# A skip term moved from VectorE to TensorE, a refolded argmax, a split load and a new order of steps

## The chip, the cores and the metric

The kernel runs on one core of a Trainium2 chip. The metric is device time of one execution in microseconds; the time of a kernel is the median of its runs. The engines are PE (TensorE), DVE (VectorE), ACT (ScalarE), POOL (GpSimd) and SP (SyncE, which only issues DMAs here). PSUM is the memory that PE writes its results to; DVE and ACT read it.

## What is computed

An input x of 2048 rows by 448 channels is normalised by rows (xn). The output is the sum of three terms:

```python
xn = layernorm(x)
return x + A(xn) + B(xn)

# A: a state-space convolution, per channel d, with 256 states n
P = exp(dt * A[d, n] * l)                    # l = 0 .. 2047
K = real(einsum("dn,dnl,dn->dl", C, P, dt * B))
A(xn) = causal_convolution(xn, K) + xn * Dskip

# B: a product-key mixture of 4096 experts, 16 heads, the best one of each head
q = einsum("nd,dhc->nhc", xn, w_q); s1 = q[..., :256] @ k1.T; s2 = q[..., 256:] @ k2.T
e = argmax(s1) * 64 + argmax(s2)             # 64 keys each; the softmax over one is 1
B(xn) = sum over heads of gelu(xn . u[e]) * v[e]
```

## The kernel before, in words

The kernel is written as streams of steps. Each step has an engine and a function that issues its instructions, and names the steps that it needs and the buffers that it takes and gives back. A string ORDER, one character a step, gives the order in which all steps are issued (`Plan.run`); each engine executes its own instructions in that order, and each waits by semaphores for what it needs. The steps carry planned costs, which issue nothing.

- **Weights.** `combine` folds w_q with the keys: 16 heads, loads wq from DRAM on SP, PE products `wc` (L889), transposes, ACT copies into W.
- **Layer norm and scores.** `ln` normalises tiles of 128 rows. `score` transposes a tile (L970), PE forms the scores of 32 lists of 64 keys (`sc`, L988 and L997), DVE takes the maximum of each list (L1012) and marks with 0 where an entry equals it (L1019, `eq`, in bf16). The argmax (stream sc_w) is then found by subtracting the ramp (64 - j)/128 from every entry (L1027) and by taking the minimum of the two halves three times, 64 to 32 to 16 to 8 entries (L1030), with a last reduction (L1033). The indices go to DRAM and come back (`ig`).
- **The convolution's kernel.** `batch` and `products` work on 8 channels at a time, 56 batches. DVE makes integer phases (L637, L641), ACT takes sines and cosines (L656 to L662, `CS`) and exponentials (L617, L619, `mg`), DVE multiplies them (L687 to L693, `zi` and `mg`). ACT's functions of different kinds need a table load when the kind changes. Then step k1 on PE sums over the states: for two groups of four channels, matmuls of 128 x 32 weights, which use a quarter of PE's columns each, into the PSUM tile `kp` (L709). Step k2 on ACT copies columns up to j0 = 63 of each group to `kt` (L717). Step k2b on DVE writes the last column, which holds time 0, as kp plus Dskip, since a skip term is an addition to the convolution's first tap (L720). `dsk` holds Dskip on partitions 0, 32, 64 and 96 and zeros elsewhere. Step k3 on PE takes the first Fourier stage of kt (`vp`, L729), and k4 on ACT copies it to VK (L733).
- **Convolution.** `conv` multiplies in the frequency domain for four chunks of channels (128, 128, 128, 64): PE `U` (L825), ACT, DVE `cp` (L835), PE `ip` (L857), ACT `tq`, stored to `t_d`.
- **Experts.** `experts`: for 64 groups, four indirect gathers by POOL bring rows of u and v (L1110, `ue`), DVE forms the dot products (L1118), ACT and DVE the gelu, PE the weighted sum `po` (L1148). ACT copies it (L1159), POOL adds it into the output in DRAM by an accumulating DMA (o_st, L1162).
- **Last stage.** `final`: `tl` is loaded from `t_d` on SP (L1188), PE applies the last stage (L1200). For the first three chunks POOL adds the result into the output (f_st, L1214). For the last chunk, SP loads the output's sums so far in one DMA, `bb` (L1180), when all 16 tiles of the experts have been stored; DVE adds the four parts (L1204), and SP stores them (L1212). SP's order at the end is three loads tl, the load bb, the fourth load tl, four stores.

The constants are loaded by SP at the start (`consts`): `dsk` by four DMAs of one row each (L332), after a POOL memset of the tile (L285).

Of the kernel before, what the change touches and what calls it, by code (L numbers as in the profile page):

```python
# [115 lines left out]
class Plan:  # L116
# [61 lines left out]
    "KKKKKSyy55TTTKhhghh7PQRZyyy5666UU56667iK9KSSTSSKKLLKK56mnjkUUUTTSSPQ59988KizdeTSTTSSAzzz!T#lT!$$5UKU5UTKK$%yyyMN5UUUTTKK"
    "iKUKK56UTSSTT955z5KUMRNZOyhSPQTTKzzz!VKUUUK#!W9$$WXSSTSUU5$%yyShhhKKK5545TTT45MNiiiiiiSThMRNZSPQz4KTTyjzhhAmnTUKklzz!SST"
    "gAAAAByyMNhhLLUKKSSYOyU#!ghhUUTTUUTUSUVmnzxzxi$$$%yyyyghhhiiiTjKMRNZOybTzxz!xSTTPQ#!UjSk$$KKKKKUcc$%yyffzzfUSTUWfMUTzz!z"  # L180
    "#!&SSTNMRZkSWXNO$fhhhhzllgKKKKKKKLLK$YYYSPQTTK$yzyz!mnTTT%yhimnKKyfSShhhgUUUU#Tz!$$SK$%fKUTTTUhhgUUhfKKfUVKzyyyyyyKzz!zx"
    "#!WhSSSPQ$$iTWK$%yyMTTiiizxSTfazxzx!dceUK#!(UK$i$SSST$%NMRZUUUTTzzSyzyyXYiiTThhhNMOyyKjiiklTS&(NMRZNOyKLPzTT!#!mnjUKUQgz"
    "klU$$$YShiihhhi%yyMNhhUSKKUTSUKzzzTTMRZNOKKULmni!#!UUVgh$$KSSThK$%WbzzKKTyzyyyzghKiihhMNSMNOTTfK!#yyTf!$UjPQRZS$zxklmnjf"
    "fU$%yyyyUUUfhWXzxzxzx!ST#!gKKKi$TKKKLLK$SSK$%yyyhhhhhhhfTTzzzffSTMNSz!TTkl&MNOKKKghhPQRTi#!fghhSS$$zzKU$%zUUfUTSSyyyyyyz"
    "!z#!KKdcebh$$UTUSSTUTTUUV$%yzzzTT!#!KK$TzxzxWmniPQSSUyyihhhy$$%yyUiiiyyUzxzxUTKUTK!#!ST$WXjkl$zSS$%yyyy&ihhmnTT(zzTzz!#!"
    "zhST$KT$zKjkgh$%yMUayyz!lmffhgUUU#!KUU$$NMRyz$%yyyyhhgNOKLKLPQMNUfffiiizzzzx!#!hhUUViiii$SMRNOyyzzz$xxxhhhhSSSTW!#!njk$T"
    "T$%yyyylmnSiihhhjkg$TT$%MNyyy&((zfflmnzzz!ffhhiiMNOSYYYWX#zzfgTT!$yz$ThPQRSz!$%yyyyUUb#iUUzzzhgST!$$$SoSz!jkUTTYYi#!hSTT"
    "Soooopzxzxzxhhdechhh$%yyyTpTTiiihj$l$%zx!i#!U$$qrpqrpooUkhfyyyy$%iqrqrzzhfffiaghhfpqpqyyyyyzlUUUUsrriizUtghhpqr!#gpqroUU"
    "!$$$jthiiVWhhhhhzzzzzusttuiiipqrpqr!#jklzz&(Yhhh%yy!pqrpoqrghhppqq$$$%IIIIIIIIghhfffffbklsrrtpqtzghhyyyiiiiWX!#!$$poqmnm"
    "nmmnn4ii$hzxzxzx4rrjjkkll%yyy5555udehihhhiimmnnzx!#siiighfhf!$$$6656jklmii%azzzfffyzyzyttu))hhgnj48899h&hghhgklm!#77777A"  # L190
    "66!$$$%yyyn*)6569885555599AAc5(zzhhiihhhihff+h6z!f*+#!z$$$%yyy)z,yhh55,yzghhg*ffbiiiiihhhdechhjiklmjn5554A55+,yg44AAByyy"
    "yyhhzz!#!xiklm$$$%yyyyhffffiiiihiin*hhg+,yjfhhgklmhhhhzxzxzx!#niizhhiijgklj!$$$%yyyyhiihfffffhhhghmhnghiabzzhdecz!zz#zzk"
    "&(lmijhhii!!$#$$z%yyyyzzznghhihhfklh!$$!#!mnijihhghkff$%yyyy$zzz$xz!#!hfghhh$%yyyy$lmfhhhiiijiingz$$%yyyyxxzklmxhizzzzzh"
    "hfnpp&(ijii!#hqrpYYklfqrpozf!$!#!$$%yyyyqqahg$$$%hhghhiirpqrpqdeczzzzzx!#ffbasrprpozxzxzxjg!$hhhii$$ttuhhkl!#yyyyqrpqrp!"
    "$$$hf%yyyy%yqhhhghhiiiiiffffq&(jklghhhhhhsrpttrpozzzzzzqii!#yyyijg!$$qrprphhfhzz!i$%#i!$hhgu$$%fffyqqhhgyzzzzzx!#!$$klsr"
    "prpofab$%iiiiyyyyyyyyyyhhhhhhttuzxzxzxqrqrhdehffffmnmnmn!#!$$$jkljgkli%yyyy&(mnmniiiiifhhhiimnsttughhjjzzzzz!#!$$$klklmn"
    "ghhzzzz!#!$$$zzzcm%yyy)%)yyyhhhhhiizxzx!#nigiiij!$$$hhihhgfff%yyklmhhnzxzxighhf!#!$$$*)+,yydefbajgklzzzzhhhhhiiiii*+hhfi"
    "%)yyym!#f&njhhghh*f(zzffklg!$$$%yyyy+zzmhhhhhiijii*klm!#,yhhzz+ngn,yiiiij!$$$%yyyyhffhiihhklghhmnzz!#!$jfffba$ghhgzxzxkl"
    "mhhiihhihhnhh$%yyyyzxijzx!ffif#!fhgklmizh$$$%yyyyhghhn&iijkgfzzz!zz#!$lmhnpp,yz$$%yyyyz!#!$$zzz$%yyyy(hiihhiihjqrpqrpohf"
    "ffhhhgz!zxqqrphhghqrpsqffbzx#!k$$$%yyyyzxzx!lhhdehhhii#!rpqrpoqiihiijgk$$$%&(tturpqrpsqzzzz!zrpyyhfhhhgf#!rpozzz!ihhgq$$"  # L200
    "$%qyyyyyyh#!hhiijkiif$$$%yyyttufzfhhhihjkihhrrppzzz!llglzxzxzxfqqs#!hhghfffftrrppozx!iihgqq#!hh$$$%iitu$$$zzzmnjklmnmnii"
    "hhhhyyyyyrrmn%&yyyy(ihhhiiiimnvovojiikliz!z#!$$$ismntjkl%wwyyyzzz!zzjkltuvmn#!$$$mnzv%ww))pprrpsrrpz!#!$$$ttusrttu%rsrrz"
    "zzz!#!$$$-*)ttusttu%&(*)*///+*+++:.;/:;:;:;<<<<,,,,")


class Kernel:
# [21 lines left out]
    def alloc(s):  # L228
# [25 lines left out]
        s.dsk = c.tile([128, D // 4], F32, name="dsk")  # L254
# [20 lines left out]
    def consts(s):  # L275
# [54 lines left out]
        def dsk():  # L330
            for c in range(4):
                s.nc.sync.dma_start(s.dsk[32 * c:32 * c + 1], io["dskip"][c:c + 1])  # L332
        s.dskip_done = p.add("c_ld", "SP", xf(4, 448), dsk, n=4, deps=[x0])
# [340 lines left out]
    def products(s, b, B, e_, c1, c2, VK, col, u):  # L674
# [24 lines left out]
        def k1():  # L699
# [3 lines left out]
            for gi in range(G):  # L703
                n = 0
                for t in range(2):
                    for ri in range(2):
                        for c in range(4):
                            m = 32 * (NB * t + 4 * gi + c)
                            s.nc.tensor.matmul(kp[32 * c:32 * c + 32, 64 * gi:64 * gi + 64], T[ri][:, 1024 + m:1056 + m],  # L709
                                               view(T[ri], m, [[512, 2], [1, 32]]), start=(n == 0), stop=(n == 3))  # L710
                        n += 1


        j0 = JB[0]

        def k2():
            s.nc.scalar.activation(B["kt"].rearrange("p (g j) -> p g j", g=G)[:, :, :j0], B["kp"].rearrange("p (g j) -> p g j", g=G)[:, :, :j0], AF.Copy)  # L717

        def k2b():
            s.nc.vector.tensor_tensor(out=B["kt"].rearrange("p (g j) -> p g j", g=G)[:, :, j0], in0=B["kp"].rearrange("p (g j) -> p g j", g=G)[:, :, j0],  # L720
                                      in1=s.dsk[:, G * b:G * b + G], op=ALU.add)
# [563 lines left out]
```

## Time and profile before

| | us |
|---|---|
| median of 3 runs | 867.54 |
| lowest and highest | 866.99, 868.65 |
| the profiled execution | 872.34 |
| its span, first to last instruction | 870.6 |

The profile is of one execution of its own, which is a little longer than the runs that were timed. A group's row has: line, engine, operation, what it writes and reads, shapes, count; then the busy time, the mean of one in ns, and the idle time of its engine just before, with what ended it. PE's tile shape stands before the shapes as rows*columns of the array. A busy PE counts each matmul from its start to its modelled end, so that overlapping ones are not counted twice.

### The profile page before, as it was taken

How to read it: one execution, taken by the hardware profiler on the slowest of the kernel's cores; microseconds unless marked ns; L12 is line 12 of the kernel's file. 1: busy time of each engine (PE TensorE's matmuls, PEld its weight loads, DVE VectorE, ACT ScalarE, POOL GpSimd, SP SyncE). 2: the span in 40 equal slices, each digit the busy share in tenths (PEclk: the TensorE clock that was granted, in tenths of full speed). 3: DMA queues.
4: the chain of work that ended last, by engine and by line, in shares of the span. 5: the costliest groups of instructions: out<-in, count | busy, mean ns of one | idle time of the engine just before them, and what ended most of it. 6: DMA issues, size and time to landing. Idle time of an engine off the chain costs nothing. (4 is left out here: it accounts for less than half of the span.)

```text
span 870.6 us, 19849 instructions
## 1 busy us (share of the span) xinstructions
PE 701.5 (81%) x7628; PEld 377.4 (43%) x7628; DVE 712.7 (82%) x1802; ACT 525.4 (60%) x962; POOL 350.6 (40%) x317
## 2 busy tenths in 40 slices
PE   3799999899999997988887475778876657877892
PEld 1234444344334433333664243456553434555662
DVE  5436999998999998988999899899988877688740
ACT  3468772552536645643578878868667866576630
POOL 1100111342444445463244267673555745444411
PEclk9999999999999999799998556699896665799995
DMA  8995622577877868879878989899889977788879
GB/s 258 311 337 202 212 56 100 172 258 214 250 226 234 299 210 249 307 208 332 284 226 259 282 198 292 276 309 275 265 288 340 251 223 209 235 247 251 248 200 178
DMA packets 145639, 212.59 MB, mean 244 GB/s; under 512 B 45512, under 2 KB 127560, under 8 KB 145480
## 3 DMA queue, kind: packets, MB, share of 16 engines
q0 software_dynamic: 29120, 124.27, 46.1%
q1 hardware_dynamic: 116424, 87.05, 33.3%
q8 instruction: 60, 0.98, 0.4%
q14 instruction: 35, 0.29, 0.1%
HBM read 181.65 MB, written 33.29 MB: 247 GB/s over the span
## 5 line engine op out<-in xcount | busy, mean ns | idle before, releaser
L1110 POOL DMA_INDIRECT ue<-in_uv_dram,ig x256 | 300.7, 1175 | 349.8 <-PE po L1148 100.9
L988 PE MATMUL sc<-W,xt 128*128 128x512 f32 x384 | 178.8, 605 | 5.6 <-ACT xt L973 4.0
L1118 DVE SCALAR_TENSOR_TENSOR ue<-ue,xr 128x448 f32<-128x448 f32 x256 | 149.7, 625 | 0.0
L988 PEld LDWEIGHTS sc<-W,xt 128*128 128x128 f32 x384 | 69.8, 191 | 92.4 <-issue 85.0
L709 PE MATMUL kp<-mg 128*32 128x64 f32 x1792 | 77.2, 248 | 25.1 <-DVE mg L693 10.3
L1148 PE MATMUL po<-ue,A 128*32 128x448 f32 x512 | 77.0, 664 | 22.5 <-DVE A L1141 21.4
L709 PE MATMUL kp<-zi 128*32 128x64 f32 x1792 | 80.9, 245 | 13.6 <-issue 13.0
L709 PEld LDWEIGHTS kp<-mg 128*32 128x32 f32 x1792 | 51.4, 125 | 49.0 <-issue 22.0
L617 ACT ACTIVATE mg<-lg 128x512 f32<-128x512 f32 x112 | 61.2, 595 | 13.7 <-PE lg L606 13.0
L693 DVE TENSOR_TENSOR mg<-mg,CS 128x1024 f32<-128x1024 f32 x56 | 68.9, 1231 | 0.0
L689 DVE TENSOR_TENSOR zi<-mg,CS 128x1024 f32<-128x1024 f32 x56 | 68.9, 1230 | 0.0
L729 PE MATMUL vp<-f,kt 128*64 128x128 f32 x448 | 45.0, 334 | 28.2 <-DVE kt L720 14.9
L709 PEld LDWEIGHTS kp<-zi 128*32 128x32 f32 x1792 | 57.1, 127 | 22.3 <-issue 21.8
L641 DVE CUSTOM_DVE_ANT_0 ph<-st,ph 128x512 uint16<-128x512 uint16 (+2 forms) x84 | 65.2, 777 | 1.6
L656 ACT ACTIVATE CS<-ph 128x1024 f32<-128x1024 int32 x56 | 61.8, 1104 | 6.0 <-DVE mg L693 4.2
L662 ACT ACTIVATE CS<-CS,halfpi 128x1024 f32<-128x1024 f32 x56 | 64.3, 1147 | 1.4
L659 ACT ACTIVATE CS<-ph 128x1024 f32<-128x1024 int32 x56 | 62.3, 1112 | 0.0
L1012 DVE TENSOR_REDUCE mx<-sc 128x8 f32<-128x512 f32 x64 | 43.7, 682 | 18.2 <-PE sc L997 10.5
L825 PE MATMUL U<-VU,g 128*64 128x128 f32 x384 | 44.9, 301 | 12.5 <-DVE cp L835 6.0
L729 PEld LDWEIGHTS vp<-f,kt 128*64 128x64 f32 x448 | 29.8, 164 | 54.9 <-DVE kt L720 16.0
L687 DVE SCALAR_TENSOR_TENSOR zi<-mg,CS 128x512 f32<-128x512 f32 x56 | 40.4, 721 | 14.9 <-ACT CS L656 10.9
L1125 ACT ACTIVATE x<-dot 128x4 f32<-128x4 f32 x64 | 13.0, 202 | 58.3 <-DVE ue L1118 57.1
(217 smaller groups left out, 1262.7 us busy)
## 6 DMA issues: line engine op xcount, KB each, us to landing
wq<-in_wq_dram SPq DMA_DIRECT2D x32, 448.0 KB
xr<-xn_d SPq DMA_DIRECT2D x64, 224.0 KB
vu_d<-vst SPq DMA_DIRECT2D x64, 112.0 KB
VU<-vu_d SPq DMA_DIRECT2D x12, 512.0 KB
t_d<-tq SPq DMA_DIRECT2D x24, 256.0 KB
tl<-t_d SPq DMA_DIRECT2D x12, 512.0 KB
ue<-in_uv_dram,ig POOLq DMA_INDIRECT x256
xx<-in_x_dram SPq DMA_DIRECT2D x16, 224.0 KB
```

Of the source, the lines that this page charges most:

```text
L641: s.nc.vector.tensor_tensor(out=rw(n, 2 * n), in0=rw(0, n), in1=o["st"][:, k, b0:b0 + 2].rearrange("p b h m x -> p (b h m x)")[:, None].to ...
L656: s.nc.scalar.activation(CS[:, 1].rearrange("p (m r x) -> p m r x", r=16, x=2), four(s.ph), AF.Sin, scale=SC)
L659: s.nc.scalar.activation(B["CS"][:, 0].rearrange("p (m r x) -> p m r x", r=16, x=2), four(s.ph), AF.Abs)
L662: s.nc.scalar.activation(B["CS"][:, 0], B["CS"][:, 0], AF.Sin, scale=-SC, bias=s.halfpi)
L689: V.tensor_tensor(out=zi[:, 512:], in0=mg[:, 512:], in1=CS[:, 1], op=ALU.mult)
L693: V.tensor_tensor(out=mg[:, 512:], in0=mg[:, 512:], in1=CS[:, 0], op=ALU.mult)
L709: s.nc.tensor.matmul(kp[32 * c:32 * c + 32, 64 * gi:64 * gi + 64], T[ri][:, 1024 + m:1056 + m], view(T[ri], m, [[512, 2], [1, 32]]), start ...
L729: s.nc.tensor.matmul(vp[64 * ri:64 * ri + 64, 128 * gi:128 * gi + 128], B["kt"][:, 64 * gi:64 * gi + 64], s.f1[:, ri], start=True, stop=True)
L988: s.nc.tensor.matmul(B["sc", q].rearrange("p a b -> p (a b)"), B["xt"][:, i], w, start=(q % 2 == 0 and i == 0), stop=(q % 2 == 1 and i == 2))
L1110: s.nc.gpsimd.indirect_dma_start(out=ue, out_offset=None, in_=s.io["uv"], in_offset=bass.IndirectOffsetOnAxis(ap=s.IDX[t][:, c, g:g + 1].b ...
L1118: s.nc.vector.scalar_tensor_tensor(Q["ue", c][:, :D], Q["ue", c][:, :D], 1.0, B["xr", c], op0=ALU.mult, op1=ALU.mult, accum_out=Q["dot"][: ...
L1148: s.nc.tensor.matmul(B["po"][32 * c:32 * c + 32, :D], Q["A"][:, c], Q["ue", c][:, D:], start=(g == 0), stop=(g == 3))
```

## The change

1. The skip term. After the matmuls of k1 for a group of four channels, four more are issued into the same PSUM columns: the weights are four rows of the identity matrix taken with a stride (4 x 32, a single 1 each), the moving operand is one column of `dsk`, which is now 4 x 112. They add Dskip to column j0 of each channel. The DVE step k2b is gone, its stream too, and k2 copies all 128 columns. k1 now also waits for dsk and for the identity matrix. The memset is gone, and one DMA loads dsk in place of four.
2. The argmax. Each minimum is now one scalar_tensor_tensor instruction that adds n/128 to the upper half and takes the minimum with the lower half. The subtraction of the ramp is left for the first 8 entries of each list, after the three minima.
3. The sums so far of the last chunk are loaded in four DMAs, one for each part of four tiles; each waits for the expert stores of its own four tiles, and each addition for its own part. SP's order at the end is three loads tl, three parts of bb, the fourth load tl, the fourth part, four stores.
4. ORDER is new throughout (the letters of the streams behind k2b move up by one).

```diff
@@ -251,7 +250,7 @@
         s.halfpi = c.tile([128, 1], F32, name="halfpi")
         s.one = c.tile([128, 1], F32, name="one")
         s.dum = c.tile([128, 1], F32, name="dum")
-        s.dsk = c.tile([128, D // 4], F32, name="dsk")
+        s.dsk = c.tile([4, D // 4], F32, name="dsk")
         s.amt = c.tile([128, 2, 4], I32, name="amt")
         s.ph = c.tile([128, 16, 2, 2, M, 2], I32, name="ph")
         s.lc = c.tile([128, 96 * NB], F32R, name="lc")
@@ -282,7 +281,6 @@
         def sets():
             s.nc.gpsimd.memset(s.halfpi, HALF_PI)
             s.nc.gpsimd.memset(s.one, 1.0)
-            s.nc.gpsimd.memset(s.dsk, 0.0)
             for h in range(2):
                 for k in range(4):
                     s.nc.gpsimd.memset(s.amt[:, h, k:k + 1], k + 2 + 6 * h)
@@ -328,9 +326,8 @@
 
 
         def dsk():
-            for c in range(4):
-                s.nc.sync.dma_start(s.dsk[32 * c:32 * c + 1], io["dskip"][c:c + 1])
-        s.dskip_done = p.add("c_ld", "SP", xf(4, 448), dsk, n=4, deps=[x0])
+            s.nc.sync.dma_start(s.dsk, io["dskip"])
+        s.dskip_done = p.add("c_ld", "SP", xf(4, 448), dsk, deps=[x0])
         ld("f1", lambda: s.f1, 131e3, 25e3)
         ld("mask", lambda: s.mask, 16e3, 30e3)
         ld("e", lambda: s.e, 197e3, 60e3)
@@ -707,18 +704,16 @@
                         for c in range(4):
                             m = 32 * (NB * t + 4 * gi + c)
                             s.nc.tensor.matmul(kp[32 * c:32 * c + 32, 64 * gi:64 * gi + 64], T[ri][:, 1024 + m:1056 + m],
-                                               view(T[ri], m, [[512, 2], [1, 32]]), start=(n == 0), stop=(n == 3))
+                                               view(T[ri], m, [[512, 2], [1, 32]]), start=(n == 0), stop=False)
                         n += 1
 
-
-        j0 = JB[0]
+                j0 = 64 * gi + JB[0]
+                for c in range(4):
+                    s.nc.tensor.matmul(kp[32 * c:32 * c + 32, j0:j0 + 1], s.ident[:4, c::4],
+                                       s.dsk[:, G * b + gi:G * b + gi + 1], start=False, stop=True)
 
         def k2():
-            s.nc.scalar.activation(B["kt"].rearrange("p (g j) -> p g j", g=G)[:, :, :j0], B["kp"].rearrange("p (g j) -> p g j", g=G)[:, :, :j0], AF.Copy)
-
-        def k2b():
-            s.nc.vector.tensor_tensor(out=B["kt"].rearrange("p (g j) -> p g j", g=G)[:, :, j0], in0=B["kp"].rearrange("p (g j) -> p g j", g=G)[:, :, j0],
-                                      in1=s.dsk[:, G * b:G * b + G], op=ALU.add)
+            s.nc.scalar.activation(B["kt"], B["kp"], AF.Copy)
 
         def k3():
             if VK["t"] is None:
@@ -731,9 +726,8 @@
 
         def k4():
             s.nc.scalar.activation(VK["t"][:, :, col:col + NB], B["vp"].rearrange("p (c k) -> p k c", k=32), AF.Copy)
-        a = p.add("s4_k1", "PE", 1340, k1, deps=[v], take=("kv", "kt"), give=("zi", "mg"))
-        a1 = p.add("s4_k2", "ACT", ac(126), k2, deps=[a])
-        a = p.add("s4_k2b", "DVE", dv(2) + 4, k2b, port=False, deps=[a1, s.dskip_done], give=("kv",))
+        a = p.add("s4_k1", "PE", 1450, k1, deps=[v, s.dskip_done, s.C["ident"]], take=("kv", "kt"), give=("zi", "mg"))
+        a = p.add("s4_k2", "ACT", ac(128), k2, deps=[a], give=("kv",))
         a = p.add("s4_k3", "PE", 510, k3, deps=[a, s.C["f1"]], take=("kv",) if VK["taken"] else ("kv", "vk"), give=("kt",))
         VK["taken"] = True
         VK["last"] = p.add("s4_k4", "ACT", ac(256), k4, deps=[a], give=("kv",))
@@ -1024,10 +1018,11 @@
 
 
             def vb():
-                s.nc.vector.tensor_tensor(out=B["eq"], in0=B["eq"], in1=s.wt[:, None, :].to_broadcast([128, 32, 64]), op=ALU.subtract)
+                s.nc.vector.tensor_tensor(out=B["eq"][:, :, :8], in0=B["eq"][:, :, :8], in1=s.wt[:, None, :8].to_broadcast([128, 32, 8]), op=ALU.subtract)
 
             def vc(n):
-                return lambda: s.nc.vector.tensor_tensor(out=B["eq"][:, :, :n], in0=B["eq"][:, :, :n], in1=B["eq"][:, :, n:2 * n], op=ALU.min)
+                return lambda: s.nc.vector.scalar_tensor_tensor(B["eq"][:, :, :n], B["eq"][:, :, n:2 * n], n / 128, B["eq"][:, :, :n],
+                                                                op0=ALU.add, op1=ALU.min)
 
             def ve():
                 s.nc.vector.tensor_reduce(out=P["cm"][:, t % 2].rearrange("p a b -> p (a b)"), in_=B["eq"][:, :, :8], axis=AX.X, op=ALU.min)
@@ -1037,7 +1032,7 @@
                 x1 = p.add("sc_a", "ACT", 8 * 196, va, deps=[x1], take=("eq",) if q == 0 else (), give=give)
             else:
                 x1 = p.add("sc_v", "DVE", dv(512), va, port=False, deps=[x1], take=("eq",) if q == 0 else (), give=give)
-        x1 = p.chain("sc_w", "DVE", [(dv(2048, 2), vb), (dv(1024, 2), vc(32)), (dv(512, 2), vc(16)), (dv(256, 2), vc(8)), (dv(256), ve)],
+        x1 = p.chain("sc_w", "DVE", [(dv(1024), vc(32)), (dv(512), vc(16)), (dv(256), vc(8)), (dv(256, 2), vb), (dv(256), ve)],
                      deps=[x1, s.wt_done], give=("eq" if t < 15 else "tq",))
         if t % 2 == 0:
             return
@@ -1175,11 +1170,15 @@
                 H["h"] = s.flat("q", "hb", 1024).rearrange("p (x e) -> p x e", e=32)
                 s.nc.sync.dma_start(H["h"], s.io["h"])
 
-            def lb():
-                H["b"] = s.flat("q", "bb", 1024).rearrange("p (t d) -> p t d", d=w)
-                s.nc.sync.dma_start(H["b"], s.io["out"][:, :, d0:].rearrange("t p d -> p t d"))
+            def lb(g):
+                def f():
+                    if g == 0:
+                        H["b"] = s.flat("q", "bb", 1024).rearrange("p (t d) -> p t d", d=w)
+                    s.nc.sync.dma_start(H["b"][:, 4 * g:4 * g + 4], s.io["out"][4 * g:4 * g + 4, :, d0:].rearrange("t p d -> p t d"))
+                return f
             h = p.add("g_h", "SP", xf(128, 4096), lh, take=("ue",), deps=[s.VKlast])
-            base = p.add("g_b", "SP", xf(2048, 4 * w), lb, hold=1500, take=("ue",), deps=[s.part[t] for t in range(16)])
+            base = [p.add("g_b", "SP", xf(512, 4 * w), lb(g), take=("ue",) if g == 0 else (), deps=[s.part[t] for t in range(4 * g, 4 * g + 4)])
+                    for g in range(4)]
         for g in range(4):
             B = {}
 
@@ -1217,7 +1216,7 @@
                       deps=[s.t_done[ck]] + ([h] if last else []), take=("ue",) + hs)
             a = p.add("g_p" if last else "f_p", "PE", 8.0 * w if last else 1000, m, deps=[a], take=("kv",), give=("ue",) if last else hs)
             if last:
-                a = p.add("g_v", "DVE", dv(4 * w), v, port=False, deps=[a, base], give=("kv",))
+                a = p.add("g_v", "DVE", dv(4 * w), v, port=False, deps=[a, base[g]], give=("kv",))
                 p.add("g_st", "SP", xf(512, 4 * w), st, deps=[a])
             else:
                 a = p.add("f_a", "ACT", ac(4 * w), v, deps=[a], give=("kv",))
```

More of the change, by code (lines that the diff above doesn't have):

```diff
@@ L178 @@
[L178 to L189, printed above, removed]
@@ new lines @@
+    "ffdelmlmTTTjkfagZTSOOOSThiihhg5S44chhghhTTTUUUUUUUUUIIIIPQRZldehhiihhihjkSSTSS4889hfhgffTSTfmVWhhgSfahhghhWXKKKKKK777TTK"
+    "KTTTKKKlmKPQRZYYxxxxx555666UU5666KKJJSSTSSKKLKKijk7569UUUTTS988TTTKdeySPQSSSi5yyyzT7K9KKL5KKTU!TUz##5#$MxNxxKUKK5AUUUTTU"
+    "T56y55SSTTi5MNRZOxU9SPQTTKyyyzKUUUVWKSSTS!zWXU5lmUU##K#$xxhhhhSKKKLL5545TTTMN5yiihiiiiSTMRZNKSPQyy44TTTUjkAAxyz!zAAABxxS"
+    "hhUig#OSTUMNhhxYKSSUUTUUTUTUVSlm##$xxxxKKKyywwghhijkTiiMRZNOxywywzbffTSPQTTjkfccK!z##ghhhS#$xx%KKKyyfUUU&STMNMRZNOUSSWyy"
@@ L206 @@
+    "yyyyywzywywyw!zzrhhghiqoqonisst!zfxppii###$xxxxffff###&hghyyyqqlmlmlmhhhhhjkiiiiihhhii$xxxx%&ununlmlmjkiiyzy!z###rsstlmi"
+    "ijk$vvxxxlmyyyzy!z###jkulmu$vvoo((qqorqqoyysstrqqyzy!z###$ysstrqqyyz!z###,)(sstrsst$%&)()*)***...---/:/:.-/:/:;;;;++++")
 class Kernel:
```

41 lines of the change are left out of this document (23 added, 18 removed).

## The prediction

> **What bounds the kernel now.** I read the page first, then busy time by stage, then the groups by line, the waits and the timeline at four places.
>
> ```profile
> span 870.6 us, 19849 instructions
> PE 701.5 (81%) x7628; PEld 377.4 (43%) x7628; DVE 712.7 (82%) x1802; ACT 525.4 (60%) x962; POOL 350.6 (40%) x317
> ```
>
> Neither TensorE (PE) nor VectorE (DVE) is full over the span, so the stages must be looked at. I cut them where PE starts its last score matmul (404 us) and where the work thins out (835 us).
>
> ```profile
> 100.00:404.00 304.00, 284.02 (x1824) 119.58 (x1823) 284.59 (x758) 150.30 (x265) 117.95 (x106) 0.97 0.69 215
> 404.00:700.00 296.00, 216.59 (x3390) 140.35 (x3392) 263.23 (x637) 224.10 (x397) 160.10 (x132) 0.78 0.89 275
> 700.00:835.00 135.00, 104.37 (x1568) 71.06 (x1560) 101.50 (x254) 83.30 (x157) 58.30 (x51) 0.83 0.77 234
> ```
>
> Columns: length, busy PE, weight loads, DVE, ACT, POOL, granted clock, DMA share, GB/s. In the **score stage** (100 to 404) PE is free 20.0 us and DVE 19.4: both are nearly full, either may set the end. In the **later stage** (404 to 835) PE is free 431 - 216.59 - 104.37 = 110.0 us, DVE 431 - 263.23 - 101.50 = 66.3: DVE is the tighter one, on a PE with a throttled clock.
>
> ```profile
> L720 DVE TENSOR_TENSOR kt<-kp,dsk 128x2 f32<-128x2 f32 x56 | 8.3, 155 | 18.1 <-ACT kt L717 18.1
> L1118 DVE SCALAR_TENSOR_TENSOR ue<-ue,xr 128x448 f32<-128x448 f32 x256 | 149.7, 625 | 0.0
> L687 DVE SCALAR_TENSOR_TENSOR zi<-mg,CS 128x512 f32<-128x512 f32 x56 | 40.4, 721 | 14.9 <-ACT CS L656 10.9 <-ACT tq L864 2.1 <-PE kp L709 1.8
> DVE kt L720 <- ACT kt L717: 12.8, 10, 3.2
> PE vp L729 <- DVE kt L720: 14.9, 10, 3.1
> ```
>
> The last two rows are waits from 404 us on: total, times, longest. The skip addition (L720) is tiny, but DVE, which runs in order, stands 18.1 us before it, and PE stands 14.9 us behind it. The dot products of the experts (L1118) never make DVE wait (0.0): gathers arrive early, so POOL and the DMAs are cover, not bound.
>
> **Part 1, the skip term.** It leaves DVE:
>
> ```profile
> 0.00:404.00 404.00, 2.39 (x16) 0.98 0.73 230
> 404.00:835.00 431.00, 5.88 (x40) 0.80 0.85 262
> ```
>
> These rows are DVE's instructions on kt alone: 2.4 us of work go before 404 and 5.9 after. Of the 18.1 us of standing, 18.1 - 12.8 = 5.3 go before and 12.8 after, if nothing else is late in its place. What is late next is whatever DVE instruction waits for ACT, as L687 does: that is a rival below. ACT's copy grows from 126 to 128 columns, nothing. The PSUM tile kp is now freed by ACT, not after a DVE turn: no loss.
>
> PE gets 56 x 8 = 448 matmuls of 4 x 32 weights and one column; the profile counts each f32 matmul twice, as it does kp's (1792 + 1792 for 56 x 32). A group of four column tiles is thus eight records, like one step of kp:
>
> ```profile
> 203.56 0.29 PE L709 MATMUL kp<-mg 128*32 128x64 f32 x8
> 203.68 0.29 PE L709 MATMUL kp<-zi 128*32 128x64 f32 x8
> 203.90 2.41 PE L988 MATMUL sc<-W,xt 128*128 128x512 f32 x5
> ...
> 683.17 0.44 PE L709 MATMUL kp<-mg 128*32 128x64 f32 x8
> 683.39 0.44 PE L709 MATMUL kp<-zi 128*32 128x64 f32 x8
> 683.80 1.28 PE L606 MATMUL lg<-lc,rt 32*128 32x512 f32 x2
> ```
>
> Step to step takes 0.11 to 0.12 us at the full clock and 0.21 in a slow stretch. But where the tile shape changes (128*32 to 128*128, or to 32*128) the next start comes after 0.22 and 0.41: a **change of tile shape** costs PE 0.11 us, or 0.20 slow. The new matmuls are 32*32 tiles in the midst of 128*32 ones. In the built order of PE's instructions the changes of shape go from 433 to 602: 50 more before the last score matmul, 119 more after it. The Trainium skill (TensorEngine Tiling (Array Packing), Key Properties) says that changing the tiling mode drains the engine; the rows agree, with the price above. Without a drain PE's two terms below would be 1.9 and 5.5 us.
>
> No row shows a one-column matmul. Bounds: nothing, and a whole kp step; I take half a step, 0.055 us a group at full clock, since the weight load remains, and between fast and slow 0.07 in the later stage, where I put a change at 0.14. With 17 batches (34 groups) before the last score and 39 (78) after: score stage 50 x 0.11 + 34 x 0.055 = 7.4 us; later stage 119 x 0.14 + 78 x 0.07 = 22.2. With whole steps it is 9.2 and 27.6; if all of it falls into PE's free time, nothing. Against it, PE's 14.9 us behind kt end.
>
> The added waits of k1 (dsk and ident loaded) are met: kp starts at 80.7, dsk was issued at 16.
>
> ```profile
> L709 PE MATMUL kp<-mg x1792: 216/219/316, 80.7 to 824.5; 128*32 128x64 f32 x200
> 16.06 3.55 SPq L332 DMA_DIRECT2D dsk<-in_dskip_dram  x4
> ```
>
> One DMA in place of four frees some 2.7 us of SP's queue there, in which the weight loads wq stand behind. I count 0; at most -2.7. The POOL memset that goes has free POOL around it: 0.
>
> **Part 2, the argmax** (16 tiles, all in or just behind the score stage).
>
> ```profile
> L1027 DVE TENSOR_TENSOR eq<-eq,wt 128x2048 bf16<-128x2048 bf16 x16 | 19.5, 1219 | 0.1
> L1030 DVE TENSOR_TENSOR eq<-eq 128x1024 bf16<-128x1024 bf16 x16 | 11.0, 687 | 0.2
> L1030 DVE TENSOR_TENSOR eq<-eq 128x512 bf16<-128x512 bf16 x16 | 6.7, 420 | 0.2
> L1030 DVE TENSOR_TENSOR eq<-eq 128x256 bf16<-128x256 bf16 x16 | 4.6, 286 | 0.3
> L691 DVE TENSOR_TENSOR mg<-mg,CS 128x512 f32<-128x512 f32 x56 | 38.3, 684 | 0.7 <-ACT CS L662 0.7
> L693 DVE TENSOR_TENSOR mg<-mg,CS 128x1024 f32<-128x1024 f32 x56 | 68.9, 1231 | 0.0
> ```
>
> Old: 1219 + 687 + 420 + 286 = 2612 ns. New: the subtraction on 256 elements (286) and three scalar_tensor_tensor instructions on bf16, which no row shows. If they run like the f32 one (721 for 512) with the f32 slope (1231 - 684 = 547 ns for 512 more): 1268 + 721 + 448, in all 2723: +0.11 us a tile, +1.8 us. If they run at the rate of the bf16 tensor_tensor: 687 + 420 + 286 + 286 = 1679, -14.9 us. I take +1.8, the same operation's row. The Trainium skill (Vector Engine (DVE) Microarchitecture Reference, 5.1) lists tensor_tensor, and not this operation, for two 16-bit results a cycle; by that it is the +1.8. No trace here shows it.
>
> **Part 3, sums so far in four parts.**
>
> ```profile
> 853.54 4.31 SPq L1180 DMA_DIRECT2D bb<-out_dram  x1
> 857.89 3.63 SPq L1188 DMA_DIRECT2D tl<-t_d  x1
> 864.15 1.09 DVE L1204 TENSOR_TENSOR bb<-po,bb 128x256 f32<-128x256 f32 x3 [22.31 <-DMA bb<-out_dram]
> 865.98 1.08 PE L1200 MATMUL po<-tl,hb 64*32 64x64 f32 x32 [4.41 <-DMA tl<-t_d]
> ```
>
> The end is a chain of SP issues: bb takes 4.31 us to issue, the last tl stands behind it and lands at 865.98. The new order is three quarters of bb, the last tl, the last quarter. The tl moves up by 4.31 / 4 = 1.1 us; but the last quarter is issued from about 860.4 to 861.5 and, landing 6.3 us after (as bb did: 857.85 to 864.15), comes at 867.8, where DVE's last addition needed its data at 867.1. So -1.1 to +0.7; I take 0. The last quarter still waits for the last expert tile's store, and the four stores stand behind it on SP; the first three additions come sooner, but not the last.
>
> **Part 4, the new order.** Counted along it, the same number of score, kp, gather and dot steps has been passed at each 25 us of planned DVE work, within a few; and 17 batches stand before the last score in both. On POOL, expert stores and chunk stores move by a few gathers; L1118's 0.0 us is the cover, and if it is gone DVE waits for gathers. One thing is countable: ACT's table loads go from 74 to 67, all seven in the score stage.
>
> ```profile
> L617 ACT ACT_TABLE_LOAD x27 | 34.6, 1283 | 0.4
> L988 PE MATMUL sc<-W,xt 128*128 128x512 f32 x384 | 178.8, 605 | 5.6 <-ACT xt L973 4.0 <-issue 1.1 <-ACT W L910 0.5
> ```
>
> That is 7 x 1.283 = 9.0 us of ACT, which is half idle there (150 of 304); PE's score matmuls wait 4.5 us for it in all. I take -1 (0 to -9). The rest of the order I put at 0, +-8: half of twice L687's 14.9 us, which an order can remove or double.
>
> **The sum.** Two queues that each wait for the other share the end; I give each a weight inverse to its free time: halves in the score stage, 0.62 DVE to 0.38 PE later. Score stage: PE +7.4, DVE -2.4 - 5.3 + 1.8 = -5.9; half of both +0.7; ACT -1. Later: PE 22.2 - 14.9 = +7.3, times 0.38 = +2.7; DVE -5.9 - 12.8 = -18.7, times 0.62 = -11.7. Together **-9.3 us**. The profiled execution took 872.34 us (span 870.6 and 1.7 around it): 863.0 there; on the median 867.54: **858.2 us**.
>
> **The rivals.**
> *PE sets the end* (slower). The 169 changes of shape and the small matmuls stay in series with PE's work: +7.4 + 7.3 = +14.7, **882.2 us**. For it: 284 of 304 us busy in the score stage. Against: 110 us free later. It decides from the point at which PE's share of the end passes 24.6 / (24.6 + 14.7) = 0.63, since DVE alone would give -24.6. The drain that the Trainium skill states (TensorEngine Tiling (Array Packing), Key Properties) is its mechanism.
> *The waits move on*: DVE stands before the next instruction that needs ACT (L687 does so now), and only the work goes. Score: (7.4 - 2.4 + 1.8) / 2 - 1 = +2.4; later: -5.9 x 0.62 + 2.7 = -1.0. **868.9 us**.
> *DVE alone sets the end*: -24.6 - 1 = **841.9 us**. Against: a score stage with PE just as full.
> *The new minimum runs at the bf16 rate*: 16.7 us less DVE work in the score stage, half of it gained: **849.8 us**.
>
> **How the numbers follow.** Forecast 0.37, PE sets 0.28, waits move on 0.18, DVE alone 0.09, bf16 rate 0.08. The forecast's own range, with the order's +-8, is 848 to 868. For 8 in 10, part of the DVE case and the top of the PE case are left out: **845 to 879**. Chances, with 0.2% (1.7 us) as what a measurement of this kernel can tell from no change: faster 0.35 + 0.05 + 0.09 + 0.08 = 0.57, same 0.11, slower 0.32.
>
> **What would show it.** No DVE instruction on kt, and PE's wait before vp then ends with ACT's kt and is shorter; eight 32*32 records behind each half of kp, spaced by about 0.11 us in and out: if far less, the PE terms fall. The new minimum at some 1270, 720, 450 ns, or 690, 420, 290. PE's last score matmul near 404 us; past 409, PE sets the end there. DVE's total near 706 us. If DVE's free time from 404 on is still some 66 us, the waits moved on. If L1118 shows waits for gathers, the order did it.

## The result, and the profile after

The changed kernel takes 894.67 us (median of 4 runs, 889.46 to 900.92), the kernel before beside it 868.1: a ratio of 1.0313, 95% interval 1.0227 to 1.0400. It is **slower by 3.1%**, where 858.2 us and a gain were forecast. One run of the kernel before, at 1114.49 us, was disturbed and is left out of the ratio. The profiled execution took 900.92 us.

From the page of the changed kernel, span and busy times, and from the view of busy time by stage, in the columns of the prediction:

```profile
span 899.2 us, 21612 instructions
PE 737.3 (82%) x8524; PEld 410.9 (46%) x8524; DVE 712.9 (79%) x1746; ACT 517.6 (58%) x955; POOL 343.9 (38%) x316
...
100.00:404.00 304.00, 279.00 (x1920) 120.82 (x1918) 270.52 (x708) 136.08 (x246) 109.72 (x102) 0.96 0.66 206
404.00:700.00 296.00, 228.68 (x3422) 149.89 (x3420) 245.63 (x570) 198.85 (x358) 140.66 (x120) 0.76 0.83 255
700.00:835.00 135.00, 101.65 (x1648) 67.83 (x1646) 109.05 (x268) 96.67 (x174) 67.80 (x58) 0.80 0.85 253
835.00:899.00 64.00, 45.49 (x981) 34.49 (x980) 27.83 (x69) 21.60 (x47) 17.99 (x15) 0.83 0.90 213
```

PE is busy 35.8 us longer (737.3 against 701.5). DVE gets through 14 us less in the score stage (270.52 where it was 284.59), 18 less in the next, and the work arrives behind 835. The last score matmul now starts at 418.5 us, not at 404.2; these are the rows of that tile, of after and of before (ns at least, in the middle and at most; first and last start):

```profile
L982 PE MATMUL sc<-W,xt x384: 592/592/1222, 31.2 to 418.5; 128*128 128x512 f32 x192
```

```profile
L988 PE MATMUL sc<-W,xt x384: 592/592/1057, 35.9 to 404.2; 128*128 128x512 f32 x192
```

The groups of the changed kernel that answer to the steps:

```profile
L712 PE MATMUL kp<-dsk,ident 4*32 4x1 f32 x896 | 37.6, 204 | 6.3 <-issue 6.1
L716 ACT ACTIVATE kt<-kp 128x128 f32<-128x128 f32 x56 | 15.2, 274 | 81.3 <-PE kp L712 56.1 <-remote 13.7 <-PE ip L851 3.4
L1123 DVE SCALAR_TENSOR_TENSOR x<-x,dot 128x4 f32<-128x4 f32 x64 | 10.2, 159 | 29.1 <-ACT x L1120 25.3 <-issue 1.8 <-ACT mg L614 1.3
L1129 DVE SCALAR_TENSOR_TENSOR th<-th,dot 128x4 f32<-128x4 f32 x64 | 10.0, 156 | 26.1 <-ACT th L1126 25.3 <-issue 0.8
L1024 DVE SCALAR_TENSOR_TENSOR eq<-eq 128x1024 bf16<-128x1024 bf16 x16 | 19.5, 1217 | 0.2
L1024 DVE SCALAR_TENSOR_TENSOR eq<-eq 128x512 bf16<-128x512 bf16 x16 | 11.0, 685 | 0.2
L1024 DVE SCALAR_TENSOR_TENSOR eq<-eq 128x256 bf16<-128x256 bf16 x16 | 6.7, 420 | 0.3
L1021 DVE TENSOR_TENSOR eq<-eq,wt 128x256 bf16<-128x256 bf16 x16 | 4.6, 288 | 0.3
```

The small matmuls, which are the last of kp, occupy PE for 37.6 us by their row. ACT's copy kt waits 56.1 us for them; before, it waited 24.5 us for kp:

```profile
L717 ACT ACTIVATE kt<-kp 128x126 f32<-128x126 f32 x56 | 15.1, 271 | 36.7 <-PE kp L709 24.5 <-PE lg L606 5.6 <-PE po L1148 2.9
```

DVE no longer waits for kt, and waits 25.3 + 25.3 us for the two ACT steps of the gelu instead (12.7 and 8.5 before: the line numbers are L1128 and L1134 there). The refolded argmax costs 1217 + 685 + 420 + 288 = 2610 ns a tile, where it cost 2612. In the timeline one batch looks so:

```profile
203.66 0.29 PE L706 MATMUL kp<-zi 128*32 128x64 f32 x8
203.89 0.29 PE L712 MATMUL kp<-dsk,ident 4*32 4x1 f32 x8
204.11 0.32 PE L706 MATMUL kp<-mg 128*32 128x64 f32 x8
...
204.47 0.29 PE L706 MATMUL kp<-zi 128*32 128x64 f32 x8
204.70 0.29 PE L712 MATMUL kp<-dsk,ident 4*32 4x1 f32 x8
204.92 0.50 PE L605 MATMUL lg<-lc,rt 32*128 32x256 f32 x4
```

From the last step of the first half to the first of the second it is 0.45 us, and 0.11 without the skip group: 0.34 us more. The second group stands before a change of shape that is there in any case, and which took 0.22 us in the kernel before (203.68 to 203.90); with the group it is 0.45, so 0.23 more. That is 0.57 us a batch at the full clock. Counted along the timeline of all matmuls, PE's tile shape changes 404 times before and 571 times after.

### The profile page after: what moved, and what is told of

The parts are those of the page before. It is cut to its first block, busy times and chain, and to the rows that moved or that the text cites. A ratio compares the mean times of both kernels' runs of the same rounds, so it can differ in the third digit from the quotient of the medians.

```text
span 899.2 us, 21612 instructions
## 1 busy us (share of the span) xinstructions
PE 737.3 (82%) x8524; PEld 410.9 (46%) x8524; DVE 712.9 (79%) x1746; ACT 517.6 (58%) x955; POOL 343.9 (38%) x316
## 4 chain that ended last, share of the span: by engine, by line
PE 45%; DVE 21%; ACT 14%; issue 9%; DMA 5%; SPq 2%; another core or an unknown queue 2%; POOL 0%; DVEq 0%; ACTq 0%; POOLq 0%
PE sc L982 9%; PE kp L706 9%; PE po L1143 4%; DVE ue L1113 4%; PE kp L712 3%; PE U L819 3%; PE ip L851 3%; PE up L745 3%; ACT CS L653 2%; PE vp L724 2%; DVE mg L690 2%; ACT CS L656 2%; PE lg L603 2%; DVE ph L638 2%
## 5 line engine op out<-in xcount | busy, mean ns | idle before, releaser
L1105 POOL DMA_INDIRECT ue<-in_uv_dram,ig x256 | 294.4, 1150 | 387.8 <-PE po L1143 119.9
L982 PE MATMUL sc<-W,xt 128*128 128x512 f32 x384 | 184.2, 621 | 8.4 <-ACT xt L967 7.5
L982 PEld LDWEIGHTS sc<-W,xt 128*128 128x128 f32 x384 | 72.2, 196 | 99.1 <-issue 87.2
L706 PE MATMUL kp<-mg 128*32 128x64 f32 x1792 | 81.6, 251 | 28.7 <-DVE mg L690 10.0
L706 PE MATMUL kp<-zi 128*32 128x64 f32 x1792 | 83.8, 247 | 11.9 <-issue 11.6
L706 PEld LDWEIGHTS kp<-mg 128*32 128x32 f32 x1792 | 49.6, 122 | 55.2 <-issue 27.4
L659 ACT ACTIVATE CS<-CS,halfpi 128x1024 f32<-128x1024 f32 x56 | 64.3, 1148 | 1.6
L706 PEld LDWEIGHTS kp<-zi 128*32 128x32 f32 x1792 | 56.4, 127 | 17.9 <-issue 17.2
L1006 DVE TENSOR_REDUCE mx<-sc 128x8 f32<-128x512 f32 x64 | 43.6, 682 | 25.7 <-PE sc L982 16.6
L716 ACT ACTIVATE kt<-kp 128x128 f32<-128x128 f32 x56 | 15.2, 274 | 81.3 <-PE kp L712 56.1
L724 PE MATMUL vp<-f,kt 128*64 128x128 f32 x448 | 42.0, 326 | 19.6 <-ACT kt L716 9.1
L684 DVE SCALAR_TENSOR_TENSOR zi<-mg,CS 128x512 f32<-128x512 f32 x56 | 39.0, 697 | 16.6 <-ACT CS L653 11.4
L851 PE MATMUL ip<-cp,e 64*128 64x256 f32 x384 | 50.0, 414 | 0.0
```

Source lines behind the costliest of these rows:

```text
L851: s.nc.tensor.matmul(Q["ip", h][:, 2 * w * x:2 * w * x + 2 * w], s.e[r, k], Q["c", x][r, :, ab, ri], start=(i == 0), stop=(i == 3))
L982: s.nc.tensor.matmul(B["sc", q].rearrange("p a b -> p (a b)"), B["xt"][:, i], w, start=(q % 2 == 0 and i == 0), stop=(q % 2 == 1 and i == 2))
L1105: s.nc.gpsimd.indirect_dma_start(out=ue, out_offset=None, in_=s.io["uv"], in_offset=bass.IndirectOffsetOnAxis(ap=s.IDX[t][:, c, g:g + 1].b ...
```

## The experiments

At the outset there were two theories. **PE**: the small matmuls lengthen PE's work, and PE sets the end. **Order**: the new order of steps makes DVE wait for ACT, whatever the skip term costs. Each chip gives the kernel before a time of its own (829.7 us on one, 867 to 871 on the others), so each result is its ratio to the kernel before on the same chip.

**The skip term on PE alone, in the old order.** The diff's edits of `dsk`, k1, k2 and the steps around them, in the kernel before; the k2b character is struck out of ORDER.

> The kernel before with the skip term on PE (four rows of weights) alone: argmax, load of the sums so far and order as before, with the steps of the removed DVE stream struck out of it. Theory PE: the 112 skip groups cost PE 0.67 us a batch, 37.6 us, and PE sets the end wherever they stand, less at most the 14.9 us that PE waited behind kt: 885 to 898 us. Theory order: the change's loss sits in the new order of the steps, so with the old order it is what the prediction's forecast said or no change: 855 to 870 us. In between, 870 to 885, both have a part.

Measured: 888.43 us, ratio 1.0273 (1.0210 to 1.0335). The old order with the small matmuls loses nearly all that the whole change loses.

**The skip term on DVE, in the new order.** The changed kernel with k1, k2 and k2b of before; in ORDER k2b stands right behind each k2.

> The changed kernel with the skip addition back on DVE (right behind ACT's copy in the order, as in 39 of the 56 places of before); new order, argmax and four loads stay. Theory PE: without the small matmuls the time goes back to the kernel before: 862 to 873 us. Theory order: it stays above 885 us, since the new order makes DVE wait for ACT's gelu steps (some 30 us more of such waits in the changed kernel's trace).

Measured: 894.93 us, 1.0326 (1.0278 to 1.0373). Taken alone this speaks for the order. But its DVE row shows where the time is lost:

```profile
L720 DVE TENSOR_TENSOR kt<-kp,dsk 128x2 f32<-128x2 f32 x56 | 8.8, 158 | 62.7 <-ACT kt L717 55.8 <-issue 6.8
```

DVE stands 62.7 us before this step, where it stood 18.1: right behind ACT's copy is a bad place for it in the new order. So the two theories were not told apart, and the skip term had to go altogether.

**No skip term, in both orders** (it is left out: no k2b, no small matmuls).

```diff
-    s.nc.tensor.matmul(kp[32 * c:32 * c + 32, j0:j0 + 1], s.ident[:4, c::4],
-                       s.dsk[:, G * b + gi:G * b + gi + 1], start=False, stop=True)
```

> Leaves the skip term out altogether: the order of before with the DVE steps on kt struck out, no small matmuls; ACT copies all 128 columns, argmax and loads as before. What DVE's part of the skip term costs in the old order. Theory that the waits go with the step: 18.1 us of standing and 8.3 us of work, most of it gained, 845 to 858 us. Theory that the waits move on to the next DVE instruction that needs ACT: only the work goes, 862 to 868. With the run that has the skip on PE in the same order (888.4) the difference is the price of the small matmuls there.

> Leaves the skip term out too: the changed kernel without its small matmuls, all else as it is (new order, refolded argmax, four loads). Theory PE, the order neutral: the same time as the old order without the skip term, within 5 us. Theory order: 12 to 28 us more than that run. Theory that the order was made for PE's added time and is only bad with the step on DVE: again equal to the old order.

Measured: 868.21 us, 0.9974 (0.9933 to 1.0015), and 866.59 us, 0.9965 (0.9924 to 1.0006); the old order again on another chip, as the base of runs below:

> The old order without any skip term (left out) once more, as the base for the three runs beside it on the same chip: 0.26% under the kernel before, as measured on another chip, within 0.5%.

866.49 us, 0.9972 (0.9938 to 1.0007). **The order is neutral** as long as no DVE step stands in it, and with it the argmax and the four loads, which the new order's run contains. The order theory falls. And the DVE step that the change removes was worth 0.3%, 2.3 us, with intervals that reach from 0.7% to nothing, though its row has 8.3 us of work and 18.1 us of standing. The work is less than the row says: DVE's total falls from 712.7 us to 708.4 and 710.6 in the two runs, since the time that a row counts for an instruction runs on after the next one has started (in the kernel before, an L1019 starts at 203.16 us and lasts 0.69, and the next instruction starts at 203.76). The waits moved to other places: over the whole span DVE is free 870.6 - 712.7 = 157.9 us before, and 857.5 - 708.4 = 149.1 and 865.2 - 710.6 = 154.6 without the step, so 3 to 9 us less and not 18. Two of the places, in the old order without it:

```profile
L684 DVE SCALAR_TENSOR_TENSOR zi<-mg,CS 128x512 f32<-128x512 f32 x56 | 39.0, 697 | 16.0 <-ACT CS L653 14.4 <-PE kp L706 1.0 <-issue 0.4
L1117 DVE SCALAR_TENSOR_TENSOR x<-x,dot 128x4 f32<-128x4 f32 x64 | 10.1, 158 | 21.8 <-ACT x L1114 16.6 <-issue 3.9 <-ACT VK L723 1.3
```

The waits for ACT's CS go from 10.9 to 14.4, those for its x from 12.7 to 16.6; the rest is spread over more groups. In the stretch from 404 to 835 DVE is free as long as before, and PE too; here is the row of the kernel before, then that of the order without skip:

```profile
404.00:835.00 431.00, 320.95 (x4954) 211.40 (x4952) 364.73 (x890) 307.40 (x553) 218.40 (x182) 0.80 0.85 262
```

```profile
404.00:835.00 431.00, 322.31 (x5010) 214.55 (x5008) 366.73 (x861) 307.90 (x557) 225.57 (x182) 0.78 0.86 260
```

DVE's free time is 66.3 and 64.3 us, PE's 110.1 and 108.7.

**The same number of small matmuls, in the tile shape of their neighbours**, in the new and in the old order.

```diff
-    s.nc.tensor.matmul(kp[32 * c:32 * c + 32, j0:j0 + 1], s.ident[:4, c::4],
+    s.nc.tensor.matmul(kp[32 * c:32 * c + 32, j0:j0 + 1], s.ident[:, 32 * c:32 * c + 32],
```

> The changed kernel with the skip matmuls in the tile shape of their neighbours: weights are 128 x 32 of the identity, dsk is again zero-padded to 128 partitions (four DMAs and a memset), so the same number of matmuls of one column, but no change of tile shape in the midst of kp. Theory PE by changes of shape: a group costs a step, 0.11 us at the full clock (0.21 throttled), in place of 0.34 (about 0.6), some 13 to 16 us in all where it was 37.6; the time falls by 10 to 24 us to 871 to 885. Theory PE by number of matmuls: the price is that of eight more instructions, whatever their shape: within 5 us of the changed kernel. Theory order: 890 or more.

> The old order with the skip term on PE in the tile shape of its neighbours (weights 128 x 32, dsk zero-padded to 128 partitions). The new order with it gave 887.2, with 20 us less busy time on PE than the four-row form. Theory PE: 16 to 18 us of small matmuls left, in place of 36 to 38, so 870 to 880. If the drains were all of the loss: 858 to 866, better than both kernels. Theory order and PE about equal: 868 to 875.

Measured: new order 887.17 us, 1.0169 (1.0092 to 1.0246); old order 885.01 us, 1.0133 (1.0085 to 1.0180). The pages of the old order, first in the four-row form and then in the neighbours' shape:

```profile
PE 731.9 (83%) x8524; PEld 403.5 (45%) x8524; DVE 710.1 (80%) x1746; ACT 526.9 (59%) x962; POOL 351.5 (40%) x316
```

```profile
PE 711.9 (80%) x8524; PEld 395.2 (45%) x8524; DVE 709.6 (80%) x1746; ACT 525.2 (59%) x962; POOL 353.5 (40%) x317
```

PE's busy time falls by 20.0 us. Along the timeline the four-row form has 585 changes of shape and the other 404, as many as the kernel before: 181 changes, 0.11 us each. The time falls by 1.4%, 12 us. So the changes of shape are about half of the loss, and the matmuls themselves the other half. Even without a change of shape the skip term is dearer on PE than on DVE.

**The argmax alone, and the four loads alone**, each in the kernel before with its part of the diff.

> The kernel before with the refolded argmax alone. The changed kernel's trace has 288 + 1217 + 685 + 420 = 2610 ns a tile in place of 2612, so by both theories nothing: 868 us, within 2. By the prediction's +0.11 us a tile it would be +0.9 to +1.8 us. If it is 3 us or more off, the order in which the scores' buffer is freed matters.

> The kernel before with the sums so far loaded in four parts and nothing else (all four at the old load's place, ahead of the last tl). Both theories: nothing, 868 within 3. If the four issues take longer on SP than the one (4.31 us) the last tl comes later, up to +3.

Measured: 866.94 us, 1.0016 (0.9979 to 1.0053), nothing; and 868.97 us, 1.0045 (1.0002 to 1.0087), which is just above nothing. In the changed order the tail keeps its length. SP's rows of after and of before, from the three loads tl on:

```profile
877.20 5.93 SPq L1187 DMA_DIRECT2D tl<-t_d  x3
883.22 6.54 SPq L1177 DMA_DIRECT2D bb<-out_dram  x3
889.87 0.45 SPq L1187 DMA_DIRECT2D tl<-t_d  x1
890.49 2.09 SPq L1177 DMA_DIRECT2D bb<-out_dram  x1
```

```profile
848.80 4.58 SPq L1188 DMA_DIRECT2D tl<-t_d  x3
```

From there to the end of the span it is 22.0 us after and 21.8 before.

**Is PE's time dear, or the path from kp to kt?** A dose of the same matmuls without the skip term, behind kp into spare columns of its PSUM tile; and a dose of DVE work that was to be of the same length (both leave the skip term out, in the old order).

```diff
+            for w in range(4):
+                for c in range(4):
+                    s.nc.tensor.matmul(kp[32 * c:32 * c + 32, G * 64 + w:G * 64 + w + 1], s.ident[:4, c::4], ...)
```

```diff
+    V.tensor_tensor(out=s.scr[:, :256], in0=mg[:, :256], in1=mg[:, :256], op=ALU.mult)
+    V.tensor_tensor(out=s.scr[:, 256:], in0=mg[:, :128], in1=mg[:, :128], op=ALU.mult)
```

> Leaves the skip term out (the old order without it, which took 0.26% less than the kernel before) and adds a dose of the same matmuls on PE that nobody waits for: after each batch's kp, four groups of four matmuls of 4 x 32 weights and one column into spare columns of the PSUM tile, 4 x 0.12 + 2 x 0.11 = 0.70 us a batch at the full clock, as the two groups of the skip term in the midst of kp take. ACT's copy to kt reads other columns. Theory occupancy (PE's own time sets the end): as slow as with the skip term on PE, +20 to +28 us, 888 to 895. Theory path (the loss is that ACT, which stands behind kt, gets kp later): +0 to +8 us.

> Leaves the skip term out too, and adds a dose of DVE work that nobody waits for: after each batch's products two multiplications into a scratch tile (256 and 128 elements, about 420 + 290 ns), 0.71 us a batch, 39.8 us, beside 38.7 us that the small matmuls added to PE's busy time. Theory that PE alone sets the end: under +8 us. Theory that DVE is as close to the end as PE, and only a removal on one of them gains nothing: +15 to +30 us. The prediction's weights (halves in the score stage, 0.62 later) would give 0.57 x 39.8 = +23.

Both ran on the faster chip, where the kernel before took 829.69 us. PE's dose: 857.06 us, 1.0350 (1.0293 to 1.0407). But ACT's copy waited for it all the same:

```profile
L715 ACT ACTIVATE kt<-kp 128x128 f32<-128x128 f32 x56 | 15.1, 270 | 30.3 <-PE kp L711 28.9 <-PE kp L706 1.4
```

L711 is the dose. The experiment failed in its aim. DVE's dose: 843.52 us, 1.0209 (1.0159 to 1.0259), 13.8 us over the kernel before. A second dose for PE stands where nobody waits for it:

```diff
+                if g < 3:
+                    for w in range(5):
+                        for c in range(4):
+                            s.nc.tensor.matmul(B["po"][32 * c:32 * c + 32, 448 + w:449 + w], s.ident[:4, c::4], ...)
```

> Leaves the skip term out (the old order without it), with a dose of the same small matmuls that nothing waits for: behind the weighted sums of the experts, in 48 of their 64 steps, five groups of four matmuls of 4 x 32 weights and one column into columns of the PSUM tile that nobody reads: 48 x (5 x 0.12 + 2 x 0.11) = 39 us at the full clock, as much as the skip term added to PE's busy time. In the other run with a dose ACT's copy kt started only 265 ns behind the dose, so it stood in the path and told nothing apart. Theory occupancy: +2.5 to +3.8% over the order without skip. Theory path (the small matmuls hurt because kt waits behind them): 0 to +1%.

Measured: 930.49 us, 1.0739 (1.0690 to 1.0787). Its rows:

```profile
L1142 PE MATMUL po<-dsk,ident 4*32 4x1 f32 x1920 | 39.7, 195 | 3.2 <-issue 3.2
L711 ACT ACTIVATE kt<-kp 128x128 f32<-128x128 f32 x56 | 15.4, 274 | 44.1 <-PE kp L706 30.6 <-PE lg L603 6.4 <-PE po L1137 5.1
```

ACT's copy waits for kp as it does without a dose (30.6 against 32.5 us), and the time is still up by 930.49 - 866.49 = 64.0 us, 7.4% of the order without skip. So **PE's time is dear without a longer path to kt**. That 39.7 us of matmuls cost 64 us was expected by neither theory. Other paths lengthened: DVE's wait for ACT's x is 42.7 us, where it was 16.6. The page also shows where part of it is: PE's total is 61.4 us above that of the order without skip (first row below; the second is this run), so its other matmuls took longer too (those of the scores 185.6 us by their row, where they took 179.7).

```profile
PE 699.1 (81%) x7628; PEld 378.6 (44%) x7628; DVE 710.6 (82%) x1746; ACT 525.1 (61%) x962; POOL 356.7 (41%) x316
```

```profile
PE 760.5 (82%) x9548; PEld 424.6 (46%) x9548; DVE 709.4 (76%) x1746; ACT 525.6 (57%) x962; POOL 349.4 (38%) x316
```

The granted clock fell too: its median over the runs is 0.874 without skip, 0.858 with the skip term on PE and 0.852 with this dose, all on one chip. Whether the lower clock is a cause of the longer time or goes with it, no run separates.

**The DVE step at its latest place in the new order.** As the run above on DVE, but each k2b as late as the PSUM buffers allow.

> The changed kernel with the skip addition back on DVE, but each of its steps as late in the new order as PSUM buffers allow (30.8 steps behind ACT's copy in the mean, 15 of 56 right behind it) in place of all right behind it, which took 3.26% more than the kernel before. The new order without any skip term took 0.35% less. Theory that the DVE step costs by where it stands: 866 to 876 us. Theory that the new order does not bear a DVE step at all: 885 or more.

Measured: 900.59 us, 1.0877 (1.0832 to 1.0922), on the faster chip. The granted clock is 0.855 here and 0.890 for the kernel before on this chip, though PE has no added work. Now PE waits for the step:

```profile
L729 PE MATMUL vp<-f,kt 128*64 128x128 f32 x448 | 43.3, 331 | 62.9 <-DVE kt L720 47.2 <-ACT VK L733 4.7 <-DVE th L1138 4.3
```

Right behind ACT, DVE stood 62.7 us; late, PE stands 47.2. Neither of the two places suits this order.

**By stage**: the skip term on PE for the last 39 batches alone, for the first 17 alone, and for all, in the old order, and the DVE dose on a second chip.

```diff
-                for c in range(4):
+                for c in range(4 if b >= 17 else 0):
```

> The skip term on PE in the old order for the last 39 batches alone (the first 17, which stand before the last score matmul, are left without it). All 56 cost 3.0% of the time, some 26 us, over the kernel without it. Theory that every PE microsecond counts alike: 39/56 and a lower clock, some 19 to 21 us over 866. Theory that PE sets the end in the score stage alone, with 110 us free later: 3 to 8 us. The prediction's weights: 22.2 x 0.38 = +8.

> The skip term on PE for the first 17 batches alone (left out for the last 39), those ahead of the last score matmul. The last 39 alone cost 1.17% of the time, some 10 us for 26 us of PE work; all 56 cost 3.0%. Theory that the two parts add: 1.8%, some 15 us for 11.4 us of PE work, so the score stage pays in full and more. The prediction's weight of a half: 6 us, 0.7%. Theory that each of the halves hides in the other (less than the sum): under 1%.

> The skip term on PE in the old order once more, beside its parts on the same chip: 2.7% over the kernel before, within 0.7%.

> The skip term on PE for the last 39 batches alone once more, on another chip than before if it falls so (there the kernel before took 829.7 us and this +0.9%). In the run with all 56 on a chip at 867 us the last score's maximum came 6 us late and the last expert step 28 us late, so 22 us fell behind the scores. Theory that the later batches cost nearly their PE time on such a chip: +2.2 to +2.8% over the order without skip (0.28% under the kernel before). Theory that the parts only hurt together: +1 to +1.4%, as on the faster chip.

> The dose of DVE work that nobody waits for, without skip term (left out), beside it: 41.6 us of DVE. On the faster chip it cost +2.1% over the kernel before. Theory that DVE is the lesser bound in the later batches: +1 to +2.3% over the kernel before, less than 0.6 of the price of the same time on PE. Theory that both are alike: +2.8% or more.

Measured, as ratio to the kernel before: the first 17 batches 1.0021 (0.9983 to 1.0058); the last 39 1.0091 (1.0053 to 1.0128) on the faster chip and 1.0119 (1.0069 to 1.0170) on another; all 56 1.0285 (1.0224 to 1.0347). Over the order without skip (0.9972, taken for the other chips too) that is 0.5%, 1.2% and 1.5%, and 3.1%. The parts sum to 1.7 to 2.0%; with intervals of 0.4 to 0.6% on each it is open whether they add up to the whole. The 2.2 to 2.8% that the theory of a full price wanted for the last 39 did not come.

The DVE dose has a ratio of 1.0018 (0.9990 to 1.0046) here, 4 us over the order without skip. Its two rows sum to 24.0 + 17.2 = 41.2 us, but DVE's total grew only from 710.6 us to 737.2:

```profile
PE 696.3 (80%) x7628; PEld 378.0 (43%) x7628; DVE 737.2 (85%) x1858; ACT 525.6 (60%) x962; POOL 361.7 (42%) x316
```

So the dose was 26.6 us of DVE's time, smaller than meant, and its price is about 0.15 us a microsecond. The skip term on PE costs 895.15 - 866.49 = 28.7 us for 36.3 us by its row, or for 43.4 us by PE's total (742.5 against 699.1): 0.65 to 0.8 us a microsecond.

On the faster chip the two are not so far apart. There the DVE dose costs 13.8 us over the kernel before, and some 16 over the order without skip if that gains 0.28% there too: for the same 26.6 us an estimate of 0.5 to 0.6 us a microsecond. The last 39 batches on PE cost 6.8 us there, some 9 by the same estimate, for 23.1 us of small matmuls: 0.3 to 0.4.

## Why the prediction was wrong, point by point

**The step that failed** is the one by which the sum was made: "Two queues that each wait for the other share the end; I give each a weight inverse to its free time", 0.62 for DVE and 0.38 for PE in the later stage. The runs show it the wrong way round on the chips on which the kernel before takes 867 to 871 us, and the change was measured at 868: 0.65 to 0.8 for PE (28.7 us for 36.3 by its row or 43.4 by its total), 0.15 for DVE (4 for 26.6). There the shorter free time of an engine did not show which one sets the end. On the faster chip DVE's price of 0.5 to 0.6 is near its weight, so the reversal is not shown for every chip.

**DVE's gain**, -24.6 us before weights, was -2.3, and can't be told from nothing. The work was put at 8.3 us by its row, where DVE's total falls by 2.1 to 4.3 without the step. Of the 18.1 us of standing 9 to 15 came back elsewhere, at L684 and L1117 among others. That is the rival *the waits move on*, and its sign came true: free time from 404 on still 64 us without the step.

**PE's 14.9 us behind kt** did not come back. The waits before vp fell, but PE's free time in the stage is the same (110.1 and 108.7).

**PE's terms**, 7.4 + 22.2 = 29.6 us, were 37.6 by the row and 35.8 by PE's total. A group of one-column matmuls costs about a whole step, not half of one: 0.34 us less two changes of 0.11 leaves 0.12. This upper end (9.2 + 27.6 = 36.8) had been worked out and not taken. A change of shape costs 0.11 us by the two shapes' runs, over both stages, where the forecast had 0.11 and 0.14.

**The score stage** is not contradicted in the old order: the first 17 batches with 17 x 0.57 = 9.7 us on PE cost 0.5%, 4.2 us, where 3.7 had been put for PE; the interval on it is as large as the cost. In the changed kernel its sign for PE, a last score matmul past 409 us, came true (418.5). The larger part of the loss falls behind the scores: the last 39 alone cost 1.5%, and 1.1% of the whole 3.1% shows in neither part alone.

**The two rivals** *PE sets the end* (882.2) and *the waits move on* (868.9) were taken as alternatives. Their mechanisms came true together: no gain on DVE to speak of, and most of PE's added time as a loss. With the prices measured afterwards, which no rival had, it is 867.54 - 2.3 + 28.7 = 893.9 us, and 894.67 was measured. The upper end of the range, 879, left out most of the PE rival, which had 0.28.

**The argmax** takes 1217 - 685 = 532 ns for 512 more elements, near the 547 of f32 and not the 267 (687 - 420) of the bf16 rival for as many, and is a little quicker than forecast (1217, not 1268): nothing, not +1.8. **The four loads** (0) and **the order** (0) hold, by the new order without skip term. The 7 table loads fewer gain nothing that can be seen.

**DVE's total** is 712.9 us, not near 706, though the step is gone. The forecast took a row's 8.3 us off a total in which that step counts for 2.1 to 4.3; and the new order's total without skip term is 713.7, 3.1 to 5.3 above the old order's. One group that grew (L514) has 1.3 us of that; the rest is open.

What stays open: why the other matmuls took longer with the dose behind `po`, what part of PE's price is the lower granted clock, and whether the parts by stage add up. No run points to a version that beats the kernel before: the best that computes the whole is the argmax alone, at the same time.

## What to carry to other kernels

An engine's free time doesn't say what an edit on it is worth. Give each engine a dose of work that nobody waits for, and weigh by what the time does; on the chips where the kernel takes 867 us or more, the one with more free time was the dear one. Measure a dose, or a step that goes, by the change of the engine's total and not by its row: rows of neighbours overlap. A wait that disappears from one instruction is a gain only when the next instruction that needs the same engine doesn't wait instead: sum the free time of the stage, not the wait. Rivals that touch different terms of a sum don't exclude each other, so add them as well.

## What the runs showed of the hardware

The same kernel with the DVE dose lost 2.1% on the chip where the kernel before took 829.7 us and 0.2% where it took 870.9. The waits of the queue show a difference, on the faster chip first and then on the other (total us, times, longest):

```profile
PEld kp L709 <- issue: 11.6, 21, 3.2
```

```profile
PEld kp L709 <- issue: 43.7, 80, 3.2
...
PE kp L709 <- issue: 20.7, 51, 0.8
```

At the many short matmuls of kp, PE stands without any cause that the profile shows; on the faster chip that is a quarter as long on the weight loads, and the row of the matmuls is missing there. Where PE loses less, DVE's time is worth more: this fits, but no run tested it. What the standing is, the runs do not tell.
